# A decode block's last weights: which rows of the first wo block come early, and how many partitions the rest is spread over

## The chip, the cores and the metric

The kernel runs on one core of a Trainium2 chip. The metric is device time of one execution in microseconds (us). All operands are fp32.

## The reference, cut to what matters

```python
xn = layernorm(x)                                  # x: 8 x 1 x 512
q = (xn @ wq) -> 8 x 32 heads x 1 x 128
scores = q . k_cache * 128**-0.5                   # 8 kv heads x 8192 keys, four q heads on each
o = softmax(scores) . v_cache                      # 8 x 32 x 1 x 128
attn = o.reshape(8, 1, 4096) @ wo                  # wo: 4096 x 512
mlp = mish(xn @ w1 + b1) @ w2                      # 512 -> 1792 -> 512
out = x + attn + mlp
```

The two caches hold 8 x 8 x 8192 x 128 numbers each: 256 MiB of keys and as much of values. All of the weights together (wq, wo, w1, w2) hold 23 MiB.

## The kernel before

**Units.** A unit is one batch row with one pair of key/value heads: 4 pairs (m = 0 to 3) times 8 batch rows, 32 units j in the order m, b. For every unit one transfer brings 8 MiB of keys and one brings 8 MiB of values, each as 128 rows of 64 KiB, one row for each partition (`load_unit`, L145). `kv` is the tile that holds them: the values at its start, two places for keys behind, which overlap.

**One turn of the loop** does, for unit j: the first half of the scores (L340), the issue of the keys of j + 1, the second half, the softmax, the weighted sum over the values of unit j - 1 (`values`, L410), the issue of the values of j, the turning of the probabilities (L379 and the VectorE work behind it), and the merge of unit j - 1 into `oT` (L427). All large transfers are issued on SyncE's queue (SP). That queue keeps the order of the program: an issue that waits holds up those behind it.

**The end of the attention.** When a pair is through, `turn_o` (L434) lays its 128 x 64 outputs out as `oX[:, m]`, and after the loop `outputs` (L541) multiplies them with the wo block of the pair. A block m is 2 MiB, seen as 128 rows of 16 KiB, row p for partition p. A row is four quarters i of 4 KiB, and a quarter is two lines of 512 outputs (h = 0, 1). So `outputs` makes 8 products for a block, n = 2i + h, that go in turn to four column groups of PE (q = n % 4).

**The tail.** After the loop SP issues the four wo blocks (L631, into the room of the values) and w2 in five pieces (L637). Behind the last values on the queue are thus 11136 KB. PE finishes the last unit, goes through `outputs` of the four blocks, `down_long` (L552), one ScalarE copy and the four `down` calls (L564); one VectorE addition (L661) and the store (L662) end the kernel.

**The early part.** To shorten the tail, a part of the first two blocks is brought during the loop, into `ws`, a tile that is free once the last wq block has been used. For the first pair `load_few(0, ...)` (L498) brings the last quarter (i = 3) of all 128 rows: 512 KB. It is folded: row r of `ws` holds that quarter of four wo rows (u = 0 to 3, 32 rows apart), four pieces of 4 KiB. The 32 rows lie on partitions 0 to 19 and 32 to 43. The list `FEW1` has eight loads, in units 22 to 25: four of five rows and four of three, the rows of one load four partitions apart. `turn_few(0)` in unit 9 makes the matching weights `oF` out of `oT` with one product (L512) and one copy (L521) for each of the two groups of partitions, and `few(0)` in unit 27 multiplies (L528), on 44 partitions. The tail then brings the other three quarters of the 128 rows, 12 KiB each, and `outputs(0)` makes 6 products (n = 0 to 5). For the second pair a smaller corner is treated in the same way (`FEW2`, units 28 to 30).

Of the kernel before, what the change touches and what calls it, by code (L numbers as in the profile page):

```python
# [13 lines left out]
P = 128  # L14
B = 8
D = 512
# [11 lines left out]
BW = 1024  # L28
CC = D // P
# [3 lines left out]
Q = P // G  # L33
# [42 lines left out]
FEWC = 256  # L76
# [6 lines left out]
def kernel(  # L83
# [12 lines left out]
    nc = tc.nc  # L96
# [8 lines left out]
    ws = const.tile([P, CC * BW], F32, name="ws")  # L105
# [7 lines left out]
    ident = const.tile([P, P], F32, name="ident")  # L113
# [13 lines left out]
    oX = const.tile([P, NP, CC, 2, B], F32, name="oX")  # L127
# [3 lines left out]
    oF = const.tile([48, 2, CC, 2, B], F32, name="oF")  # L131
# [25 lines left out]
    rows = wq.rearrange("j p f -> (j p f)").rearrange("(m p f) -> m p f", m=NP, p=P)[0]  # L157
# [335 lines left out]
    def load_few(m, p, k, q, slot):  # L493

        rows = wo[4 * m : 4 * (m + 1)].rearrange("u p f -> (u p f)")
        rows = rows.rearrange("(u q i f) -> q u i f", u=4, i=4, f=BW)
        n = FEWC if m else BW
        nc.sync.dma_start(  # L498
            ws[p : p + 4 * k - 3 : 4, 4 * n * slot : 4 * n * (slot + 1)].rearrange(
                "p (u f) -> p u f", u=4  # L500
            ),
            rows[q : q + 4 * k - 3 : 4, :, 3, BW - n :],
        )

    def turn_few(m):

        o = oT.rearrange("p h b -> p (h b)")
        n = H2 * B
        parts = ((0, 12, 0, 0), (0, 12, 12, 1), (32, 8, 24, 0)) if m else ((0, 20, 0, 0), (32, 12, 20, 0))
        for p, r, lo, slot in parts:  # L510
            t = M[p : p + r, 384 + n * slot : 384 + n * (slot + 1)]
            nc.tensor.matmul(t, ident[:, 4 * lo + 3 : 4 * (lo + r) : 4], o, start=True, stop=True)  # L512
            if m:
                nc.vector.tensor_copy(
                    oF[p : p + r, 1].rearrange("p u h b -> p (u h b)").rearrange(
                        "p (s u b) -> p s u b", s=2, u=CC
                    )[:, slot],
                    t.rearrange("p (u h b) -> p u h b", u=CC, h=2)[:, :, 1],
                )
            else:  # L520
                nc.vector.tensor_copy(oF[p : p + r, 0].rearrange("p u h b -> p (u h b)"), t)  # L521
# [12 lines left out]
            )  # L534

    def outputs(m, t):
        for n in range(2 * (3 if m == 0 else CC)):
            i, h = divmod(n, 2)
            q = n % G
            c = D - FEWC if (m, n) == (1, 7) else D  # L540
            nc.tensor.matmul(  # L541
                H[Q * q : Q * q + B, :c],
                oX[:, m, i, h],
                t[:, n * D : n * D + c],
                start=False,
                stop=False,
            )
# [33 lines left out]
    for j in range(UNITS):  # L581
        b = j % B
        more = j // B + 1 < NP

        k = k_t.pop(j)
# [14 lines left out]
        if j == B + 1 or j == 2 * B + 1:  # L600
            turn_few(j // B - 1)
# [7 lines left out]
        for m, rows in enumerate((FEW1, FEW2)):  # L609
            for p, k, q, at, slot in rows:  # L610
                if j == at:
                    load_few(m, p, k, q, slot)
# [13 lines left out]
    w_o = [kv[:, 4096 * m : 4096 * (m + 1)] for m in range(NP)]  # L626
    for m in range(NP):
        rows = wo[4 * m : 4 * (m + 1)].rearrange("u p f -> (u p f)")
        rows = rows.rearrange("(p f) -> p f", p=P)
        n = (3 * BW, 4 * BW - FEWC)[m] if m < 2 else 4 * BW  # L630
        nc.sync.dma_start(w_o[m][:, :n], rows[:, :n])  # L631
    w2_rows = w2.rearrange("j p f -> (j p) f").rearrange("(q i) f -> q (i f)", i=W2R)
    w2_t = []
    parts = ((0, G), (G, 8), (8, 11), (11, 13), (13, 14))
    for lo, hi in parts:
        t = kv[:, W2_AT + lo * D : W2_AT + hi * D]
# [5 lines left out]
    for m in range(NP):  # L642
        if m == 1:
            merge(UNITS - 1, os)
            turn_o(NP - 1)
        outputs(m, w_o[m])
# [3 lines left out]
    for g in range(G):  # L650
# [4 lines left out]
            start=True,  # L655
            stop=False,
# [44 lines left out]
```

## Time and profile before

| what | us |
|---|---|
| median of three runs | 1309.39 |
| lowest and highest | 1309.39, 1309.89 |
| span of the profiled execution, first to last instruction | 1307.7 |
| PE busy | 991.8 |
| VectorE busy | 357.6 |
| ScalarE busy | 39.2 |

The profile records the span of the profiled execution; what lies around it is the difference to the timed runs, 1.7 us to their median. Busy times of engines overlap and don't add up to the span. "PE" counts matmuls, "DMA" the 16 engines that carry the transfers; a line such as L631 is a line of the kernel's source. A queue line gives packets, megabytes and the share of the time of 16 DMA engines. In the table by stretches of time, the last two columns are the busy share of the DMA engines and the GB/s moved, where a packet counts in the stretch in which it starts.

### The profile page before, as it was taken

The numbers are of one execution on the slowest core, as the hardware profiler recorded it, in microseconds if no ns is written. First come the engines' busy times: TensorE is split into PE (matmuls) and PEld (weight loads), VectorE is DVE, ScalarE is ACT, GpSimd is POOL, SyncE is SP. The second block draws the span as 40 slices with busy tenths as digits, with TensorE's granted clock in tenths as the row PEclk, the third lists the DMA queues.
The fourth block names the chain that finished last, engine by engine and source line by source line (L and its number), as shares of the span: only waits on it lengthen the run. The fifth ranks groups of instructions, "written<-read, shape, count | busy, mean of one in ns | idle before, by whom it ended". The sixth has DMA issues, their size and how long they took to land.

```text
span 1307.7 us, 11247 instructions
## 1 busy us (share of the span) xinstructions
PE 991.8 (76%) x5090; PEld 348.8 (27%) x5090; DVE 357.6 (27%) x676; ACT 39.2 (3%) x89; POOL 2.3 (0%) x10
## 2 busy tenths in 40 slices
PE   6967876768878778776877877687696687777686
PEld 4222222223322222222322222232242222222222
DVE  3352122231233332123221322311323321323321
ACT  1000000000000000000000000000000000000000
POOL 0000000000000000000000000000000000000000
PEclk9999888888888788888888888798888998888898
DMA  9999999999999999999999999999999999999998
GB/s 404 444 421 442 425 439 428 433 435 430 434 433 432 435 432 436 424 442 429 434 434 429 438 425 442 423 440 427 437 426 436 435 428 436 432 432 429 433 435 337
DMA packets 11927, 561.80 MB, mean 430 GB/s; under 512 B 1364, under 2 KB 1632, under 8 KB 2152
## 3 DMA queue, kind: packets, MB, share of 16 engines
q1 hardware_dynamic: 11712, 560.03, 99.2%
q10 hardware_dynamic: 168, 1.06, 0.3%
q8 instruction: 40, 0.66, 0.2%
q14 instruction: 7, 0.06, 0.0%
HBM read 561.01 MB, written 0.07 MB: 429 GB/s over the span
## 4 chain that ended last, share of the span: by engine, by line
DMA 77%; PE 23%; issue 0%; ACT 0%; SPq 0%; DVE 0%
DMA kv<-in_v 57%; DMA kv<-in_kT 18%; PE o L410 15%; PE s L340 7%; DMA kv<-in_w 2%; PE x L379 1%; PE x L304 0%; ACT qr L311 0%; PE o L564 0%; PE m L427 0%; SPq L155 0%; SPq L159 0%; DVE os L661 0%; DVE rt L387 0%; PE m L383 0%
## 5 line engine op out<-in xcount | busy, mean ns | idle before, releaser
L340 PE MATMUL s<-kv,wk 128*64 128x512 f32 x2048 | 502.8, 654 | 177.0 <-DMA kv<-in_kT 169.9
L410 PE MATMUL o<-kv,pt 128*32 128x512 f32 x2048 | 267.6, 682 | 56.6 <-DMA kv<-in_v 56.6
L340 PEld LDWEIGHTS s<-kv,wk 128*64 128x64 f32 x2048 | 164.0, 151 | 492.1 <-issue 403.5
L352 DVE TENSOR_REDUCE nm<-s 128x1 f32<-128x512 f32 x32 | 22.1, 692 | 511.6 <-PE s L340 511.6
L379 PE MATMUL x<-e,perm 128*128 128x512 f32 x256 | 130.7, 658 | 2.0 <-ACT qr L311 2.0
L410 PEld LDWEIGHTS o<-kv,pt 128*32 128x32 f32 x2048 | 70.5, 123 | 227.8 <-issue 175.1
L418 DVE TENSOR_SCALAR os<-o,isel 128x128 f32<-128x128 f32 x32 | 11.2, 351 | 281.5 <-PE o L410 281.5
L390 DVE STREAM_TRANSPOSE tr<-x 128x512 f32<-128x512 f32 x128 | 79.2, 676 | 3.2 <-PE x L379 3.2
L379 PEld LDWEIGHTS x<-e,perm 128*128 128x128 f32 x256 | 50.6, 208 | 75.5 <-issue 72.9
L323 DVE TENSOR_TENSOR wk<-qr,mask 128x1024 f32<-128x1024 f32 (+1 forms) x33 | 62.8, 1902 | 18.8 <-ACT qr L311 18.7
L371 ACT ACTIVATE e<-s,nmx 128x512 f32<-128x512 f32 x32 | 22.0, 687 | 1115.4 <-DVE nmx L368 1115.4
L399 DVE TENSOR_TENSOR pt<-tr 64x512 f32<-64x512 f32 x64 | 43.9, 686 | 1.6
L395 DVE TENSOR_TENSOR tr<-tr 128x1024 f32<-128x1024 f32 x32 | 39.2, 1225 | 1.1
L420 DVE SCALAR_TENSOR_TENSOR os<-o,isel,os 128x128 f32<-128x128 f32 x96 | 33.7, 351 | 3.4
L353 PE MATMUL m<-ident,nm 128*1 128x128 f32 x32 | 8.6, 270 | 25.3 <-DVE nm L352 25.3
L364 PE MATMUL m<-ident,nx 1*128 1x1 f32 x32 | 7.0, 217 | 19.8 <-DVE nx L358 19.8
L304 PE MATMUL x<-qT,tr 128*128 128x64 f32 x128 | 19.3, 315 | 3.0 <-ACT qr L311 2.7
L304 PEld LDWEIGHTS x<-qT,tr 128*128 128x128 f32 x128 | 18.1, 226 | 6.2 <-ACT qr L311 3.3
L353 PEld LDWEIGHTS m<-ident,nm 128*1 128x1 f32 x32 | 2.5, 79 | 53.5 <-DVE nm L352 53.5
L374 DVE TENSOR_SCALAR lsel<-rsel,l 128x8 f32<-128x8 f32 x32 | 7.4, 231 | 28.8 <-ACT e L371 28.8
L427 PE MATMUL m<-hsel,os 128*128 128x8 f32 x64 | 10.9, 242 | 5.6 <-DVE rt L387 5.6
L427 PEld LDWEIGHTS m<-hsel,os 128*128 128x128 f32 x64 | 10.8, 189 | 15.2 <-DVE rt L387 7.2
(107 smaller groups left out, 174.6 us busy)
## 6 DMA issues: line engine op xcount, KB each, us to landing
ws<-in_wq SPq DMA_DIRECT2D x3, 2048.0 KB
kv<-in_wo SPq DMA_DIRECT2D x2, 2048.0 KB
kv<-in_w SPq DMA_DIRECT2D x1, 3584.0 KB
kv<-in_w SPq DMA_DIRECT2D x2, 1024.0 KB
kv<-in_wo SPq DMA_DIRECT2D x1, 1920.0 KB
kv<-in_wo SPq DMA_DIRECT2D x1, 1536.0 KB
ws<-in_wq ACTq DMA_DIRECT2D x1, 1024.0 KB
ws<-in_wq SPq DMA_DIRECT2D x1, 1024.0 KB
```

Of the source, the lines that this page charges most:

```text
L304: nc.tensor.matmul(X[:, half, k * 64 : (k + 1) * 64], wide[:, half * 8 + k], qT, start=True, stop=True,)
L323: nc.vector.tensor_mul(w[:, i : i + n], q[:, i : i + n].to_broadcast([P, n, 2, NH * G, REP]), mask.rearrange("p (o d k r) -> p o d k r", o ...
L340: nc.tensor.matmul(S[64 * c : 64 * (c + 1), :], w[:, i].rearrange("p d k h -> p (d k h)"), kk[:, i, c, :], start=(part == 0 and n == 0), s ...
L352: nc.vector.tensor_reduce(nm, S, axis=AX.X, op=ALU.max, negate=True)
L371: nc.scalar.activation(e, S, AF.Exp, bias=nmx, accum_out=l)
L379: nc.tensor.matmul(X[:, g], perm[:, g], e, start=True, stop=True)
L390: nc.vector.transpose(tr.rearrange("p (l t) c -> p t l c", t=TL)[:, tl], X.rearrange("p g (t q l) -> p t l g q", t=TL, q=PP)[:, tl],)
L395: nc.vector.tensor_add(t[:, :, 0], t[:, :, 0], t[:, :, 1])
L399: nc.vector.tensor_add(pt8[half, :, :, d * REP : (d + 1) * REP].rearrange("p c y h -> p y c h"), t[:, 0], t[:, 1],)
L410: nc.tensor.matmul(O[Q * q : Q * (q + 1), :], pt8[:, c, TL * l : TL * (l + 1), :].rearrange("p t h -> p (t h)"), vt[:, 512 * n : 512 * (n ...
L420: nc.vector.scalar_tensor_tensor(os, O[:, DH * i : DH * (i + 1)], isel[:, i : i + 1], os, op0=ALU.mult, op1=ALU.add)
L427: nc.tensor.matmul(M[:, 168 : 168 + H2], os, hsel, start=True, stop=True)
```

## The change

The early part of the first block is cut the other way. Instead of the last quarter of all 128 rows it is now the last 32 rows (96 to 127) in full: one 16 KiB row of wo for each row of `ws`, on the same partitions of `ws`, in the same eight loads. The rest of the block, brought in the tail, is then 96 rows of 16 KiB on partitions 0 to 95, in place of 128 rows of 12 KiB. `turn_few(0)` makes four products of 16 columns for each of the two groups (one for each quarter i), with one copy each as before. `outputs(0)` makes 8 products on 96 partitions in place of 6 on 128. The bytes of both parts stay the same: 512 KB early, 1536 KB late. The other blocks, the second pair's early part and w2 are untouched.

```diff
     def load_few(m, p, k, q, slot):
         rows = wo[4 * m : 4 * (m + 1)].rearrange("u p f -> (u p f)")
+        if m == 0:
+            rows = rows.rearrange("(p f) -> p f", p=P)[3 * Q :]
+            nc.sync.dma_start(ws[p : p + 4 * k - 3 : 4, :], rows[q : q + 4 * k - 3 : 4, :])
+            return
         rows = rows.rearrange("(u q i f) -> q u i f", u=4, i=4, f=BW)
-        n = FEWC if m else BW
+        n = FEWC
...
     def turn_few(m):
...
             t = M[p : p + r, 384 + n * slot : 384 + n * (slot + 1)]
+            if m == 0:
+                for i in range(CC):
+                    nc.tensor.matmul(
+                        t[:, 2 * B * i : 2 * B * (i + 1)],
+                        ident[:, 4 * lo + i : 4 * (lo + r) : 4],
+                        o[:, 3 * 2 * B :],
+                        start=True,
+                        stop=True,
+                    )
+                nc.vector.tensor_copy(oF[p : p + r, 0].rearrange("p u h b -> p (u h b)"), t)
+                continue
...
     def outputs(m, t):
-        for n in range(2 * (3 if m == 0 else CC)):
+        k = 3 * Q if m == 0 else P
+        for n in range(2 * CC):
...
-                oX[:, m, i, h],
-                t[:, n * D : n * D + c],
+                oX[:k, m, i, h],
+                t[:k, n * D : n * D + c],
...
     for m in range(NP):
...
-        n = (3 * BW, 4 * BW - FEWC)[m] if m < 2 else 4 * BW
-        nc.sync.dma_start(w_o[m][:, :n], rows[:, :n])
+        k = 3 * Q if m == 0 else P
+        n = 4 * BW - FEWC if m == 1 else 4 * BW
+        nc.sync.dma_start(w_o[m][:k, :n], rows[:k, :n])
```

(P is 128, Q 32, CC 4, B 8, D 512, BW 1024, FEWC 256.)

## The prediction

> **What bounds the kernel now.** I read the page's totals first, then the queues, then the chain of work that ended last.
>
> ```profile
> span 1307.7 us, 11247 instructions
> ...
> DMA  9999999999999999999999999999999999999998
> GB/s 404 444 421 442 425 439 428 433 435 430 434 433 432 435 432 436 424 442 429 434 434 429 438 425 442 423 440 427 437 426 436 435 428 436 432 432 429 433 435 337
> ...
> q1 hardware_dynamic: 11712, 560.03, 99.2%
> ...
> DMA 77%; PE 23%; issue 0%; ACT 0%; SPq 0%; DVE 0%
> ```
>
> The 16 DMA engines are busy from the first slice to the last but one; the queue of SP alone fills 99.2% of their time. One engine moves 560.03 MB / 16 / (0.992 x 1307.7 us) = 27.0 GB/s, and the rate is the same whether keys, values or weights come. PE is in the chain for 23% only because a score or a value product releases room for the next transfer. So the kernel lasts as long as its transfers, and bytes are what counts, unless an engine is made to run slower or to wait.
>
> The end of the chain of waits, from the landing of the last values on, and the sizes on the queue behind the last values:
>
> ```profile
> 1277.74 26.10 DMA kv<-in_w
> 1303.84 0.04 issue
> 1303.88 0.62 PE o L564 x16
> ```
>
> ```profile
> kv<-in_wo SPq DMA_DIRECT2D x2, 2048.0 KB
> ...
> kv<-in_w SPq DMA_DIRECT2D x2, 1024.0 KB
> kv<-in_wo SPq DMA_DIRECT2D x1, 1920.0 KB
> kv<-in_wo SPq DMA_DIRECT2D x1, 1536.0 KB
> ...
> kv<-in_w SPq DMA_DIRECT2D x1, 768.0 KB
> ...
> kv<-in_w SPq DMA_DIRECT2D x1, 512.0 KB
> ...
> kv<-in_w SPq DMA_DIRECT2D x1, 256.0 KB
> ```
>
> Four blocks of wo and five pieces of w2 make 11136 KB; in 26.10 us that is 437 GB/s, the full pace. The tail is one unbroken stream, and the 1536 KB of the first block are its first piece. Whatever that piece loses, the last piece of w2 loses too, if the engine that ends last is among the losers. Which engines have slack is seen in the table by stretches (the last two columns are DMA share and GB/s):
>
> ```profile
> 1294.00:1298.00 4.00, 1.90 (x16) 0.38 (x16) 0.00 (x0) 0.00 (x0) 0.00 (x0) 1.00 0.94 389
> 1298.00:1302.00 4.00, 2.51 (x48) 1.00 (x48) 0.00 (x0) 0.59 (x1) 0.00 (x0) 1.00 0.76 317
> ```
>
> In the second stretch a quarter of the engines' time is gone: about four of the 16 have ended by 1298 us, the other twelve run to the last landing at 1303.84 us. Those twelve have next to no slack, so a loss that is spread over half of the engines or more can't miss them.
>
> **The change part by part.**
>
> *PE and VectorE.* In unit 9 `turn_few(0)` stands here (start, duration, engine and line):
>
> ```profile
> 403.23 0.31 PE L512 MATMUL m<-oT,ident 128*20 128x64 f32 x2 [1.98 <-DVE oX L443]
> ...
> 403.91 0.29 PE L512 MATMUL m<-oT,ident 128*12 128x64 f32 x2 [0.37 <-DVE oF L521]
> ...
> 411.92 0.65 PE L340 MATMUL s<-kv,wk 128*64 128x512 f32 x2 [3.22 <-DMA kv<-in_kT]
> ```
>
> Each product is two instructions. The change has 8 products for 2: 12 instructions more. One behind the other at 0.31 us a pair they cost 1.9 us, overlapped less. VectorE's copies stay two. Behind them on PE wait the turning (L379) and the merge, and all of that ends 3.22 us before the scores, which wait for their keys. So 1.9 us is hidden; without that cover it would be 1.9 us.
>
> In the tail, `outputs(0)` goes from 6 products to 8:
>
> ```profile
> 1287.36 1.90 PE L541 MATMUL h<-kv,oX 128*8 128x512 f32 x12
> ...
> 1295.92 1.90 PE L541 MATMUL h<-kv,oX 128*8 128x512 f32 x16 [1.96 <-DMA kv<-in_wo]
> ```
>
> The 12 instructions of block 0 take as long as the 16 of block 3, since the products go to four column groups and either count needs two rounds. I take 0; one product row more at the most, 0.4 us, and PE waits 1.96 us for a wo block afterwards, which covers it. The first block is at the head of a stream that starts at 1277.74 us and takes 3.6 us of it; were it 7.3 us late, at 1288.6 us, PE would start on it 1.3 us late, and that too fits into the 1.96 us. `few(0)` keeps its shapes.
>
> *SP's queue.* The eight early issues remain, with one piece a row in place of four:
>
> ```profile
> 954.76 1.53 SPq L498 DMA_DIRECT2D ws<-in_wo  x2
> 974.26 0.34 SPq L145 DMA_DIRECT2D kv<-in_kT  x1
> ```
>
> Two issues take 1.53 us and the next one waits until 974.26 us, so a cheaper or dearer issue changes nothing.
>
> *The early transfers.* Same bytes, same rows of `ws`, 32 pieces of 16 KiB for 128 of 4 KiB. The stretch without such loads and the stretches with them:
>
> ```profile
> 900.00:940.00 40.00, 30.66 (x152) 10.15 (x150) 11.91 (x19) 0.78 (x2) 0.00 (x0) 0.87 0.99 428
> 940.00:980.00 40.00, 34.99 (x187) 14.43 (x184) 10.33 (x19) 1.95 (x4) 0.00 (x0) 0.91 1.00 434
> 980.00:1020.00 40.00, 28.69 (x140) 9.73 (x138) 10.13 (x18) 0.78 (x2) 0.00 (x0) 0.87 1.00 432
> ```
>
> 434 and 432 GB/s with 4 KiB pieces in the stream, 428 without: there is no loss by small pieces to win back. A bound from above: the 0.8% of the time that the queue doesn't fill is 10.5 us; put down to its 11712 packets alone, the 128 packets fewer (96 early, 32 late) save 10.5 x 128 / 11712 = 0.1 us. I take 0.
>
> *The late transfer of block 0.* This is the part that can cost. Nothing is added in bytes: 1536 KB is 98304 bytes for each of 16 engines, 98304 / 27.0 = 3.64 us, before and after. What is new is where it goes. Every large transfer of the trace has 128 rows, one for each partition; this one has 96, and partitions 96 to 127 get nothing. No row of before shows such a transfer, so I bound it.
>
> From below: if an engine's pace doesn't depend on where it writes, 0 us.
>
> [...]
>
> [...] So the late engines lose between 3.6 and 7.3 us; the stream behind is unbroken and doesn't give it back. I take the middle, **5.5 us**.
>
> [...]
>
> The sum: 0 + 0 + 0 + 5.5. Span 1307.7 + 5.5 = 1313.2 us; with the 1.7 us by which the median of the runs, 1309.39, lies above that span: **1314.9 us**.
>
> **The rivals.**
>
> [...]
>
> *No lanes: only bytes count.* This rival ends not slower. If the limit sits at the engines or at the source, 16 engines carry 98304 bytes each as before and the time stays at 1309.4 us, 0.1 us less at best. It decides as soon as two engines can write into the same part of the memory at full pace. For it: the pace is the same for all sources. [...]
>
> *Faster.* Only if the 4 KiB pieces hold back the engines that end last by more than the totals show, by over 2.6 us in 32 rows. The two stretches at 434 and 432 GB/s speak against it.
>
> *The change doesn't do what it says:* the 96 rows are cut again into the pieces of before. Then 1309.4 us.
>
> **How the numbers follow.** What a measurement here can tell from no change is about 0.2%, 2.6 us. Chances: lanes shared 0.58 (1314.9; its own range 1312.0 to 1319.0), owners kept 0.18 (1310.6), bytes only 0.17 (1309.4), faster 0.04, cut as before 0.03. Slower by over 0.2% is the first, 0.58; within it the second, third and last, 0.38; faster 0.04. The range of 8 in 10 has to hold most of the first and the second and part of the third: 1309.3 to 1318.5.
>
> **What would show it.** If lanes are shared, the last wait for w2 grows from 26.10 us to about 31, while the stretch in which the first block travels moves fewer GB/s than the 432 or so of the rest, and everything ahead of 1277 us stays. [...] With bytes only, the chain stays as it is. The queue's packets should fall by 128, from 11712 to 11584; if they don't, the rows are cut otherwise. L512 should have 12 instructions more and L541 four, with the scores after unit 9 starting when their keys land, as before. I would be wrong altogether if the stretches ahead of the tail changed, since I see nothing there that costs or saves.

## The result, and the profile after

The changed kernel takes 1319.66 us (median of five runs, 1318.12 to 1320.37); the kernel before, beside it, 1309.39 us. The ratio is 1.0078, with a 95% interval of 1.0067 to 1.0088: 10.3 us slower. The direction is that of the forecast; the size, 5.5 us, is half of it, and the range ended at 1318.5. The profiled execution took 1319.53 us, 1.7 us over its span.

From the page of the changed kernel: the span, the pace of the transfers in 40 equal slices, and SP's queue.

```profile
span 1317.8 us, 11279 instructions
...
GB/s 402 443 436 424 436 438 418 443 434 431 434 434 435 428 434 441 417 446 426 429 442 431 428 438 426 436 436 428 433 431 437 431 433 430 432 436 434 426 330 307
...
q1 hardware_dynamic: 11584, 560.03, 99.2%
```

The packets fall by 128 and the bytes are equal, so the transfers were cut as the diff says. The pace is that of before in 38 slices; only the last two, 33 us each, fall to 330 and 307 GB/s, from 435 and 337. The share of busy time doesn't show it: 99.2% both times. An engine that is held up counts as busy.

The end of the chain of waits, after (start, duration, what):

```profile
1247.59 35.65 DMA kv<-in_v
...
1283.26 30.63 DMA kv<-in_w
```

And the last values in the same view of the kernel before:

```profile
1247.77 29.95 DMA kv<-in_v
```

The wait for w2 grew by 4.5 us (26.10 before). But more was lost earlier, in the last values: the wait for them grew by 5.7 us, and they landed 5.5 us later (1283.26 us for 1277.74). They are ahead of the changed transfer on the queue, and the change doesn't touch them. The table by stretches of time shows how (the last two columns are DMA share and GB/s), after:

```profile
1262.00:1266.00 4.00, 4.00 (x31) 1.27 (x24) 0.89 (x3) 0.00 (x0) 0.00 (x0) 1.00 1.09 463
1266.00:1270.00 4.00, 3.65 (x23) 1.82 (x25) 1.75 (x5) 0.00 (x0) 0.00 (x0) 1.00 1.28 434
1270.00:1274.00 4.00, 0.44 (x10) 0.00 (x0) 3.92 (x6) 0.00 (x0) 0.00 (x0) 0.89 1.15 262
1274.00:1278.00 4.00, 0.00 (x0) 0.00 (x0) 0.23 (x2) 0.00 (x0) 0.00 (x0) 0.50 0.79 195
1278.00:1282.00 4.00, 0.00 (x0) 0.00 (x0) 0.00 (x0) 0.00 (x0) 0.00 (x0) 0.50 0.68 164
1282.00:1286.00 4.00, 2.62 (x16) 0.76 (x20) 0.00 (x0) 0.00 (x0) 0.00 (x0) 0.50 1.00 215
1286.00:1290.00 4.00, 4.00 (x40) 1.21 (x36) 0.00 (x0) 0.00 (x0) 0.00 (x0) 0.91 0.98 219
1290.00:1294.00 4.00, 4.00 (x38) 1.09 (x30) 1.40 (x4) 0.00 (x0) 0.00 (x0) 1.00 0.93 359
1294.00:1298.00 4.00, 2.73 (x26) 0.94 (x25) 1.03 (x5) 0.00 (x0) 0.00 (x0) 1.00 1.01 428
...
1270.00:1290.00 20.00, 7.06 (x58) 1.97 (x52) 4.14 (x7) 0.00 (x0) 0.00 (x0) 0.66 0.92 211
```

And the 20 us in the kernel before:

```profile
1270.00:1290.00 20.00, 14.19 (x102) 4.55 (x101) 6.96 (x14) 0.00 (x0) 0.00 (x0) 0.83 0.96 407
```

For 20 us the whole stream runs at half pace, 211 GB/s for 407. What is missing, 20 us x 196 GB/s = 3.9 MB, takes 9.1 us at 430 GB/s. Some 0.6 us more of the 10.1 us lie in the four us behind, at 359 GB/s where the kernel before has 419 (an estimate: 60 GB/s x 4 us, at 430 GB/s). The trace's packet records say whose time it is. A packet of 64 KiB takes 2.42 us in the undisturbed stream, one of 16 KiB 0.614 us. I add up what the packets take beyond that; divided by the 16 engines it is the stream's loss:

```
changed kernel, packets that start from 1264 to 1300 us    beyond the usual, all engines
64 KiB (last values)                          66 packets    64.3 us
16 KiB (block 0, then block 2)               273 packets    64.1 us
15 KiB (block 1)                             128 packets    31.4 us
sum / 16                                                    10.0 us
the same sum in the kernel before                            0.1 us
```

The first engine enters block 0 at 1269.4 us, and the values of all the others slow down as soon as three engines are there, at 1270.3 us (3.3 to 4.9 us a packet for 2.42). Six tenths of the loss (64.3 and 31.4 of 159.8 us) aren't in the packets of the 96 rows at all.

### The profile page after: what moved, and what is told of

It is laid out like the page before. It is cut to its first block, busy times and chain, and to the rows that moved or that the text cites. A ratio compares the mean times of both kernels' runs of the same rounds, so it can differ in the third digit from the quotient of the medians.

```text
span 1317.8 us, 11279 instructions
## 1 busy us (share of the span) xinstructions
PE 984.1 (75%) x5106; PEld 346.7 (26%) x5106; DVE 357.6 (27%) x676; ACT 39.2 (3%) x89; POOL 2.4 (0%) x10
## 3 DMA queue, kind: packets, MB, share of 16 engines
q1 hardware_dynamic: 11584, 560.03, 99.2%
## 4 chain that ended last, share of the span: by engine, by line
DMA 77%; PE 22%; issue 0%; ACT 0%; SPq 0%; DVE 0%
DMA kv<-in_v 39%; DMA kv<-in_kT 36%; PE s L340 12%; PE o L410 9%; DMA kv<-in_w 2%; PE x L379 0%; PE x L304 0%; ACT qr L311 0%; PE o L580 0%; PE m L427 0%; SPq L155 0%; SPq L159 0%; DVE os L678 0%; DVE rt L387 0%; PE m L383 0%
## 5 line engine op out<-in xcount | busy, mean ns | idle before, releaser
L410 PE MATMUL o<-kv,pt 128*32 128x512 f32 x2048 | 256.8, 659 | 61.9 <-DMA kv<-in_v 61.9
```

The source lines that it names most:

```text
L410: nc.tensor.matmul(O[Q * q : Q * (q + 1), :], pt8[:, c, TL * l : TL * (l + 1), :].rearrange("p t h -> p (t h)"), vt[:, 512 * n : 512 * (n ...
```

## The experiments

Two theories stood against each other. "Lane by lane" is the author's assumption behind the prediction's 3.6 to 7.3 us: an engine that writes a row off its own lane, the partitions that it is assumed to fill when a load has 128 rows, loses, and so does the engine whose lane that is. The prediction's chances call this "lanes shared". No run shows lanes: the trace gives the start, the size and the duration of a packet, but neither its partition nor the number of its engine. "Whole stream": as long as rows such as the 96 are on the way, all 16 engines slow down. A rival lay outside the late transfer: the early rows, or the products. In the diffs of the probes below, the data are read by nobody.

### One part at a time: late128, late96

```diff
# late128, against the changed kernel
-        nc.sync.dma_start(w_o[m][:k, :n], rows[:k, :n])
+        nc.sync.dma_start(w_o[m][:, :n], rows[:, :n])
# late96, against the kernel before
-        nc.sync.dma_start(w_o[m][:, :n], rows[:, :n])        # n = 3 * BW for m == 0
+        nc.sync.dma_start(w_o[m][:k, :n], rows[:k, :n])      # k = 96, n = 4 * BW for m == 0
```

> The changed kernel with one thing put back: the late part of the first block comes in 128 rows of 16 KiB (the early 32 rows come a second time), 512 KB more than before. Early rows and products stay as changed. If the loss sits in the 96-row transfer (both theories of the stream), only the bytes are left: 1309.4 + 512 KB at 430 GB/s = 1310.6 us. If it sits in the early rows or in the products, it stays: about 1320 us and 1.2 us more.

> The kernel before with one thing changed: the late part of the first block comes in 96 rows of 16 KiB on partitions 0 to 95. Early rows and products stay as before, so the product of the first block takes part of its weights from what lay there. Both theories of the stream: the whole loss, 1319.7 us. Early rows or products as the cause: 1309.4 us.

late128: 1310.53 us, ratio 1.0008 (0.9999 to 1.0018). late96: 1320.17 us, ratio 1.0079 (1.0064 to 1.0094). The same 20 us, late128 first:

```profile
1270.00:1290.00 20.00, 14.15 (x119) 4.94 (x121) 7.30 (x16) 0.00 (x0) 0.00 (x0) 0.83 0.97 411
```

```profile
1270.00:1290.00 20.00, 7.10 (x50) 2.44 (x52) 5.38 (x9) 0.00 (x0) 0.00 (x0) 0.66 0.96 210
```

The late transfer alone makes the loss, and neither early rows nor products have a part in it. A third more bytes in 128 rows costs 1.1 us where 96 rows cost 10.

### A quarter of the size: short96

```diff
+        if m == 0:
+            nc.sync.dma_start(w_o[0][: 3 * Q, n:], rows[: 3 * Q, n:])
         nc.sync.dma_start(w_o[m][:, :n], rows[:, :n])
```

> The kernel before with a short transfer more, ahead of the first block: 96 rows of 4 KiB on partitions 0 to 95, 384 KB, 0.9 us of bytes, data that nobody reads. Theory 'whole stream' (as long as any engine is in such a transfer, all 16 run at half pace; the loss is the distance between the engines, about 7 us, and the length of the transfer): 0.9 + 7 + 0.9, 1318.2 us. Theory 'lane by lane' (an engine loses in proportion to the bytes that it writes off its own lane): 0.9 + 10.3 / 4, 1312.9 us.

1313.52 us, ratio 1.0029 (1.0018 to 1.0041): 4.1 us more, of which 0.9 are bytes. Neither number; the "whole stream" theory misses by more. Its window is 12.5 us long, and the pace in it is 307 GB/s rather than half:

```profile
1269.50:1282.00 12.50, 2.76 (x26) 0.96 (x30) 4.94 (x8) 0.00 (x0) 0.00 (x0) 0.67 0.93 307
```

With rows of a quarter the engines pass through one after the other, with gaps between them: no such row is on the way from 1271.7 to 1273.5 us or from 1274.9 to 1275.8 us. So the distance between the engines isn't lost in full. The next runs ask what a few rows cost, and where.

### Eighteen forms in mid-stream: probes, probes2, probes3

```diff
# PROBES of probes: unit, rows of wo, partitions of ws (with BW, 4 KiB of each row)
+    (6, slice(0, 29, 4), slice(0, 29, 4)),
+    (8, slice(64, 93, 4), slice(64, 93, 4)),
+    (10, slice(0, 8), slice(0, 8)),
+    (14, slice(0, 61, 4), slice(0, 61, 4)),
+    (16, slice(0, 32), slice(0, 32)),
+    (18, (slice(0, 96), slice(0, BW)), (slice(0, 96), slice(0, BW))),
# PROBES of probes2
+    (6, slice(64, 69, 4), slice(64, 69, 4)),
+    (8, slice(8, 13, 4), slice(8, 13, 4)),
+    (10, slice(64, 77, 4), slice(64, 77, 4)),
+    (14, slice(0, 64), slice(0, 64)),
+    (16, (slice(0, 128), slice(0, BW)), (slice(0, 128), slice(0, BW))),
+    (18, (slice(32, 128), slice(0, BW)), (slice(32, 128), slice(0, BW))),
# PROBES of probes3
+    (6, slice(0, 9, 8), slice(0, 9, 8)),
+    (8, slice(0, 65, 64), slice(0, 65, 64)),
+    (10, slice(0, 5, 4), slice(0, 5, 4)),
+    (14, (slice(0, 112), slice(0, BW)), (slice(0, 112), slice(0, BW))),
+    (16, (slice(0, 127, 2), slice(0, BW)), (slice(0, 127, 2), slice(0, BW))),
+    (18, (slice(0, 128), slice(0, BW)), (slice(0, 128), slice(0, BW))),
# all three
+        for at, src, dst in PROBES:
+            if j == at:
+                nc.sync.dma_start(ws[dst], wo_rows[src])
```

> [...] Bytes alone, at one engine's pace: 4.6 us, 1314 us, the first form nothing beyond that. Whole stream: each of the last five costs some 5 to 8 us, with the stretch at about 215 GB/s: about 1345 us. Lane by lane: each costs at most its own length once more, 4 us in all: 1318 us. [...]

> Six more small transfers in mid-stream, in the places of the last six. [...]

> Six more forms in the same places, to find how little it takes. [...] Unit 14, 112 rows of 4 KiB on partitions 0 to 111; unit 16, 64 rows of 4 KiB on every second partition; unit 18, 128 rows of 4 KiB. [...] Unit 10 and unit 18 nothing. [...]

The loss of the stream by each, from the packet records as above:

```
rows x KiB   partitions                      loss, us
 8 x 16      0 to 28, step 4                 0.00
 2 x 16      0, 4                            0.00
 2 x 16      0, 8                            0.07
 2 x 16      0, 64                           0.09
 2 x 16      8, 12                           0.46
 2 x 16      64, 68                          0.49
 4 x 16      64 to 76, step 4                0.75
 8 x 16      64 to 92, step 4                1.33
 8 x 16      0 to 7                          1.56
16 x 16      0 to 60, step 4                 1.55
32 x 16      0 to 31                         5.73
64 x 16      0 to 63                         6.79
96 x 4       0 to 95                         3.12
96 x 4       32 to 127                       3.13
112 x 4      0 to 111                        2.93
64 x 4       0 to 126, step 2                0.00
128 x 4      0 to 127 (twice)                0.03, 0.07
```

The totals of the runs, one each, were 1328.15, 1327.31 and 1318.10 us. The first lies between its two forecasts, 1318 and 1345. It fits the table: 13.3 us of losses and 4.6 us of bytes (an estimate, for an engine that carries a part of every form at 27.0 GB/s) make 1327.3. Estimated in the same way (6.4 and 4.7 us of bytes), the other two come to 1327.3 and 1317.3. Three stretches of the first, with the first form, the second and the 32 rows:

```profile
306.00:316.00 10.00, 6.03 (x34) 1.95 (x34) 1.57 (x5) 0.78 (x2) 0.00 (x0) 0.97 1.02 439
384.00:398.00 14.00, 9.71 (x53) 2.89 (x52) 1.57 (x5) 0.78 (x2) 0.00 (x0) 0.88 1.02 398
...
704.00:726.00 22.00, 12.77 (x68) 3.77 (x68) 1.57 (x5) 0.78 (x2) 0.00 (x0) 0.77 0.99 313
```

The third run of them, with 112 rows and then with 64 rows on every second partition:

```profile
622.00:634.00 12.00, 6.18 (x30) 1.96 (x30) 1.58 (x5) 0.78 (x2) 0.00 (x0) 0.90 0.95 306
700.00:714.00 14.00, 10.80 (x60) 3.61 (x60) 1.57 (x5) 0.78 (x2) 0.00 (x0) 0.98 1.00 431
```

Three things follow. **Two rows can cost next to nothing**: 0.00 us on partitions 0 and 4, 0.07 us on 0 and 8, 0.09 us on 0 and 64. With 0 and 8, two packets of 64 KiB took 2.73 and 2.85 us and the others some 0.03 us more than usual. **The same two rows elsewhere slow everyone**: 0.46 us on partitions 8 and 12, 0.49 us on 64 and 68. With 64 and 68 the rows were on the way for 0.8 us, and 16 packets of 64 KiB of the engines' own stream took 2.75 to 3.00 us. Two engines that lose the 0.6 us of a row each would cost the stream below 0.1 us (an estimate: 2 x 0.6 us over 16 engines), so "lane by lane" doesn't account for it. And **it isn't the count of rows**: 112 rows of 4 KiB on partitions 0 to 111 cost 2.93 us, 64 rows evenly over all partitions 0.00 us. Which engine takes which row isn't in the trace, so what sets the cheap places apart is not shown.

### Nothing beside it: alone, align_before, align_after

```diff
# alone, against the kernel before
     nc.sync.dma_start(out, res)
+    for first, k in ((0, P), (0, 96), (0, 64), (32, 96)):
+        n = 96 * 4 * BW // k
+        nc.sync.dma_start(kv[first : first + k, :n], flat.rearrange("(p f) -> p f", p=k))
# align_before and align_after, against the kernel before and the changed one
+    nc.sync.dma_start(ws[64:65, :16], kv[:1, K_AT[0] : K_AT[0] + 16])
     w_o = [kv[:, 4096 * m : 4096 * (m + 1)] for m in range(NP)]
```

> The kernel before with four transfers of 1536 KB more after the result has been stored, one after the other, nothing else on the way: 128 rows of 12 KiB; 96 rows of 16 KiB on partitions 0 to 95; 64 rows of 24 KiB on 0 to 63; 96 rows on 32 to 127. The first: 3.7 us of bytes. [...]

> The kernel before, with a copy of 64 bytes out of the last values ahead of the wo blocks on the same queue: the blocks are issued once the last values have landed, so that all 16 engines start on them together. The stream has a hole of some 2 us: about 1311.5 us. It is the base for the next run.

> The changed kernel with the same copy: the 16 engines start the 96 rows together, the last values are through. If a row off its lane has its price whatever else flows, the distance to the run above stays 10 us: 1321.5 us. If the loss is what the 96 rows take from the values and from the blocks beside them (the engines 7 us apart), it shrinks to what crowding costs, 1.2 to 3.7 us: 1313 to 1315 us.

In the run "alone", from the first packet to the end of the last: 128 rows 5.1 us, 96 rows 7.3 us, 64 rows 8.2 us, 96 rows on 32 to 127 7.2 us. The stretches of the last three:

```profile
1313.00:1320.40 7.40, 0.00 (x0) 0.00 (x0) 0.00 (x0) 0.00 (x0) 0.00 (x0) 0.50 0.87 213
...
1322.50:1330.80 8.30, 0.00 (x0) 0.00 (x0) 0.00 (x0) 0.00 (x0) 0.00 (x0) 0.50 0.86 190
...
1332.60:1340.00 7.40, 0.00 (x0) 0.00 (x0) 0.00 (x0) 0.00 (x0) 0.00 (x0) 0.50 0.89 213
```

The pace of the 96 rows alone, 213 GB/s, is that of the stream beside them, 211. But alone the half pace lasts 7.3 us, and the loss against 128 rows is 2.2 us. (The 128 rows took 5.1 us where 3.7 were expected; a start and an end without a stream around them are in all four durations.)

align_before took 1314.73 us (ratio 1.0041, 1.0026 to 1.0056), more than the 1311.5 expected: the hole in the stream was longer, and its chain ends with PE. align_after took 1317.15 us (1.0059, 1.0043 to 1.0076). The distance is 2.4 us in place of 10.3. By the packets' excess it is 3.9 less 1.0, 2.9 us, which no end on PE blurs. So with all engines in the 96 rows together, three quarters of the loss go. (The 1.2 us in the forecast of align_after is the author's estimate, and no run shows it; the runs gave the 2.4 and 2.9 us.)

### The same bytes on other partitions: own_late, own_all

```diff
# own_late, against the changed kernel
+        if m == 0:
+            nc.sync.dma_start(w_o[0][::2], rows[: 2 * Q])
+            nc.sync.dma_start(w_o[0][1::4], rows[2 * Q : 3 * Q])
+            continue
# own_all: early rows
+            nc.sync.dma_start(ws[3::4], rows[3::4])
# own_all: late rows
+            nc.sync.dma_start(w_o[0][::2], rows[::2])
+            nc.sync.dma_start(w_o[0][1::4], rows[1::4])
# own_all: weights, a 0/1 mask by partition in place of the products of turn_few(0)
+            nc.vector.tensor_scalar(oE, flat, pick[:, 0:1], None, op0=ALU.mult)
+            nc.vector.tensor_scalar(flat, flat, pick[:, 1:2], None, op0=ALU.mult)
```

> The changed kernel with the same 96 rows of 16 KiB, the same bytes and the same engines' share, but on other partitions: 64 rows on every second partition and 32 rows on every fourth from 1 on, two transfers. The product of the first block reads other rows than it should. [...] If what costs is rows off their engine's lane, the loss goes: 1309.5 us. If 96 rows of 16 KiB or a late part with fewer than 128 rows cost by themselves, it stays at about 1320 us; half of it would go if only one of the two transfers fits.

> [...] Off-lane theory: no loss. The early 512 KB are now on all 16 engines, 32 KiB or 1.2 us each, in place of five engines; if the 12 engines that end last are mainly those without early rows, they end up to 1.2 us later: 1309.4 to 1310.7 us; if the five were the last, up to 1.2 us earlier than 1309.4.

own_late: 1309.40 us, ratio 1.000 (0.999 to 1.001), where the changed kernel has 1.0078. The 20 us once more:

```profile
1270.00:1290.00 20.00, 14.19 (x116) 4.94 (x118) 6.96 (x14) 0.00 (x0) 0.00 (x0) 0.83 0.95 406
```

96 rows of 16 KiB, on other partitions, cost nothing. They come as 64 and 32 rows, but that split doesn't save them: 64 rows on 0 to 63 and 32 rows on 0 to 31 cost 6.79 and 5.73 us in the probes. So the cause is which partitions the rows lie on. By what way it matters is not shown. own_all, a full version of the change's idea, takes 1310.66 us, ratio 1.0009 (0.9999 to 1.0019): the loss is gone, but nothing is won against the kernel before. No version run here beats it.

## Why the prediction was right or wrong

**What bounds the kernel** held. The tail is one unbroken stream, and what it lost showed at the end in full: 10.0 us by the packets, 10.1 us in the span.

**PE and VectorE** held. `turn_few(0)` in unit 9, after:

```profile
403.28 0.49 PE L518 MATMUL m<-oT,ident 128*20 128x16 f32 x8 [1.98 <-DVE oX L443]
...
404.15 0.37 PE L518 MATMUL m<-oT,ident 128*12 128x16 f32 x8 [0.37 <-DVE oF L525]
...
411.44 2.79 PE L340 MATMUL s<-kv,wk 128*64 128x512 f32 x12 [2.42 <-DMA kv<-in_kT]
```

Twelve instructions more took 0.26 us more on PE (0.86 for 0.60), below the 1.9 us allowed, and the scores still waited 2.42 us for their keys. In the tail, the products of block 0:

```profile
1291.92 1.91 PE L557 MATMUL h<-kv,oX 96*8 96x512 f32 x16
```

1.91 us for its 16 instructions, 1.90 for the 12 of before: no longer, as taken.

**SP's queue** held: in unit 23 the two early issues take 1.43 us for 1.53, and the next one waits until 973.26 us.

**The early transfers** held: 128 packets fewer, late128 at 1.1 us by its bytes alone, and no change of pace before the tail.

**The late transfer** is the step that failed. The prediction said: "So the late engines lose between 3.6 and 7.3 us". The lower end is the 3.64 us of the transfer once more, for rows at half pace; the upper end adds as much again for engines that others hold up. Both were the author's estimate from the assumption of lanes, and no run shows that term or the 5.5 us taken from it. What the runs showed in its place: the lower end was near in size, 64.1 / 16 = 4.0 us in the 16 KiB packets, though the packets don't tell a shared lane from a slowing of all engines. The rest was more than the 3.64 us that the upper end adds: 64.3 and 31.4 us of engine time, 6.0 us of the stream, went in the values and in block 1, which are loads of 128 rows and run at full pace where no such transfer is on the way. The assumption lets only those engines lose that meet in a lane; in the runs the whole stream lost: 0.46 to 0.49 us by two rows on partitions 8 and 12 or 64 and 68, and about half the pace with 96 rows, 211 GB/s for 407. How long that lasts is then what counts. Of the engines, 7 us apart, the first few held back the values of the others, which came later to the 96 rows for it, and the last ones held back block 1. So half pace lasted for 20 us rather than the 7.3 us of the transfer alone. Aligned, the loss was 2.4 to 2.9 us, and there the prediction's 3.6 would have been near.

The statement that everything ahead of 1277 us stays was wrong for the same reason: the last values land 5.5 of the 10 us later. The wait for w2, at 30.63 us, came out near the "about 31" forecast, but that is luck: it holds only the smaller half of the loss.

**The rivals.** "Owners kept", 1310.6 us in the chances, was an estimate from the same assumption, 1.2 us that no run shows; the half pace excludes it. "Only bytes count" is excluded by late128 against late96, 1310.53 us with more bytes against 1320.17 us. Of lanes the runs show nothing. What they show is that a row's partition decides: own_late takes all of the loss away, 1309.40 us for 1319.66. Why two rows slow the stream on some partitions and not on others stays open: the trace doesn't record where a packet is written.

## What to carry to other kernels

In a stream that keeps all transfer engines busy, the shape of one transfer can cost others more than itself: here 6.0 of the 10.0 us were lost in loads of 128 rows. What cost next to nothing here were loads of 128 rows (0.03 and 0.07 us), 64 rows on every second partition (0.00 us), these together with 32 rows on every fourth (own_late, ratio 1.000), and eight rows four partitions apart from partition 0 on (0.00 us; from partition 64 on 1.33 us): give a load one of these forms, or measure it in the stream. Price another form by the time during which it is on the way, with the whole stream at about half pace (an estimate, from 211 GB/s for 407 and from 0.49 us lost in 0.8 us; the two rows on 0 and 8 lost only 0.07 us). Engines that have come apart stretch that time, here from 7.3 to 20 us, though a short transfer doesn't lose the whole distance (short96: 3.2 us beyond its bytes, with the engines about 7 us apart); its own bytes say little. Read the pace by stretches rather than the busy share: in the 20 us at 211 GB/s the share was 0.92, and 0.96 at 407 GB/s.

## What the runs showed that was not expected

- Two rows of 16 KiB cost the stream 0.46 us on partitions 8 and 12 and 0.49 us on 64 and 68, but 0.00 to 0.09 us on 0 and 4, 0 and 8, 0 and 64.
- 96 rows of 16 KiB cost 10.3 us in the stream, 2.2 us alone, and nothing on partitions in even steps.
- The engines of one queue come apart. In the kernel before, the first had its last values at 1270.0 us, the last at 1277.2 us. The early loads, of two to five rows, may have a part in that; but the three wq blocks, 128 rows each and ahead of all early loads, show it too: by their packets, the last engine was 2.0, 3.4 and 5.9 us behind the first near 229, 543 and 858 us (an estimate: first start to last end, less eight packets of 0.614 us). Why is open.
